# Stores in 8 KB rows, a written order for every engine, and 29 gate products on GpSimd in a scan and mixture-of-adapters kernel

## The chip, the core and the metric

The kernel runs on one core of a Trainium2 chip. The core has TensorE (PE, matrix products; PEld is its loading of weights), VectorE (DVE), ScalarE (ACT), GpSimd (POOL), SyncE (SP, which here only issues DMAs) and 16 DMA engines. The metric is the device time of one execution in microseconds (us), the median of several runs. A profile is one execution; its span goes from the first to the last instruction.

## The reference

Eight sequences of 6400 rows of 128 numbers go through a linear recurrence. The resulting 51200 rows go through a mixture of eight rank-16 adapters, of which the two with the largest gate logits are used.

```python
for t in range(S):                       # a, b: [8, 6400, 128]
    h = a[:, t] * h + b[:, t]
    out[:, t] = h
...
x = out.reshape(51200, 128)
logits = x @ w_gate                      # [51200, 8]
topk = np.argpartition(-logits, K, axis=1)[:, :K]      # K = 2
w = softmax of the two selected logits
...
delta[mask] += w[mask, k, None] * (x[mask] @ A[e]) @ B[e]
...
return x + delta
```

Everything is float32 outside; 26.2 MB each of a, b and output.

## The kernel before

The 51200 rows are cut into 100 units of 512 rows. Each unit goes through these steps; the letters are the names of the operations in the code.

- **ld** (SyncE): a and b come in by DMAs of two units each, 128 partitions by 4 KB, into rings `a_in` and `b_in` of eight slots. A slot is loaded again when the transposes of its units are done.
- **AB** (TensorE, function `transposes`): eight float32 transposes each of a and b on half the partitions, into `pA` and `pB`, so that time runs along the free dimension.
- **aev** (ScalarE, L491): `pA` is copied to `a_st`. Then **scan** (VectorE, L510): one scan instruction makes x for 512 steps, in float16, into the ring `xT`, and starts from the last column of the unit before.
- **L** (TensorE): gate logits, four matmuls of 8 columns into a part of the bank `pTL`. For a group of up to four units **lev** (ScalarE) copies them out, VectorE reduces (L618, L646: the two largest), GpSimd does the elementwise steps (L625 to L674), and **sig** (ScalarE) makes the gate weights `g`.
- **Z** (TensorE): x times all A, into `pZ`. **mul** (L729): Z times the gate, on VectorE from `pZ`, or, for the units that `POOL_MULS` names, on GpSimd from `z_sb`, to which ScalarE has copied Z first (**zev**, L715). Result `zw`, float16.
- **T** (TensorE): transposes `zw` into the other part of `pTL`. **tev** (ScalarE, L786) copies it to `zwT`.
- **R** and **D** (TensorE, function `delta`): into `pO`, x itself (as weights against an identity) and then `zwT` times B.
- **oev** (ScalarE, some of the last ones VectorE, L821): `pO` goes to one of the `NOUT` = 24 slots of `outt`.
- **st** (SyncE): two units' slots go out in one DMA of 128 rows of 4 KB; units 0, 1 and 96 to 99 one at a time, in rows of 2 KB. So that a row of the output holds eight consecutive input rows, R reads every eighth column of x over two units (`x_rows`) and tev rearranges its columns to match (`evacuated`). A store also waits for the scan 22 units later (`HOLD`), so that loads go first.

The tiles that limit how far the steps can run ahead: `xT` holds 16 units, `zwT` two tiles of two units, `pB`, `pZ` and `pO` two each, `pA` one.

The order of instructions on each engine is made by `_Plan.schedule` at build time: a list scheduler with an estimated cost of each operation, offsets for its kind (`KEY`) and a tolerance (`SLACK`). It also picks the engine where there is a choice. Each engine runs its list strictly in order, and `run` (L188) puts semaphore waits ahead of an operation where another engine's work is needed. All DMAs but those of the constants are in SyncE's list. In the steady part the planner comes to T, L, D, Z, R, AB on TensorE for every unit.

Of the kernel before, what the change touches and what calls it, by code (L numbers as in the profile page):

```python
# [5 lines left out]
ALU = mybir.AluOpType  # L6
ACTF = mybir.ActivationFunctionType
F32 = mybir.dt.float32
# [4 lines left out]
KEY = {  # L13
    "AB": -228.9, "aev": 79.1, "scan": 140.1, "L": -12.2, "lev": -63.6, "gate": 83.5, "sig": 69.7, "Z": 27.8,
    "mul": -75.3, "zev": 6.2, "T": -117.7, "tev": 38.1, "R": 189.8, "D": 29.2, "oev": 168.4,
}
SLACK = {"pe": 20.0, "dve": 20.0, "act": 0.0, "pool": 60.0, "sp": 120.0}
# [3 lines left out]
POOL_MULS = (2, 10, 4, 2)  # L21
# [3 lines left out]
WIDE = 100  # L25
SOLO = (2, 4)
FUSE = (100, 100)
WIDE8 = 460.0
RING = 8
XR = 16  # L30
NOUT = 24
TAIL = 10
FILLS = 1


class _Op:


    def __init__(self, name, engs, kind, unit, cost, emit, deps, dma, bank, mode):
        self.name = name  # L40
        self.engs = engs
        self.eng = engs[0]
        self.kind = kind
        self.unit = unit
        self.cost = cost
        self.emit = emit
        self.deps = deps
        self.dma = dma
        self.bank = bank
        self.mode = mode  # L50
        self.signal = False
        self.done = None
# [7 lines left out]


# [30 lines left out]
class _Plan:  # L92


    def __init__(self, sems, offset, slack):
        self.sems = sems
        self.offset = offset
        self.slack = slack
        self.ops = {}
        self.order = {e: [] for e in sems}  # L100

    def add(self, name, eng, kind, unit, cost, emit, deps=(), dma=None, bank=None, mode=None):

        engs = (eng,) if isinstance(eng, str) else eng
        cost = cost if isinstance(cost, dict) else {e: cost for e in engs}
        self.ops[name] = _Op(name, engs, kind, unit, cost, emit, list(deps), dma, bank, mode)

    def schedule(self, first, link, landing, switch):
        ops = self.ops
        users = {n: [] for n in ops}  # L110
        left = {}
        for op in ops.values():
            op.deps = [ops[d] for d in dict.fromkeys(op.deps) if d in ops]
            left[op.name] = len(op.deps)
            op.key = op.unit + self.offset.get(op.kind, 0.0)
            op.quick = min(c[0] for c in op.cost.values())
        for op in ops.values():
            for d in op.deps:
                users[d.name].append(op)
        begin, end = {}, {}  # L120
        cand = {e: [] for e in self.sems}
        free = {e: first for e in self.sems}
        bank = {}
        mode = None
        for op in ops.values():
            if not left[op.name]:
                for e in op.engs:
                    cand[e].append((0.0, op))
        todo = len(ops)
        while todo:  # L130
            found, soonest = [], {}
            for e, c in cand.items():
                for x in c:
                    op = x[1]
                    t = max(free[e], x[0])
                    if op.bank:
                        for o in bank.get(op.bank, {}).values():
                            if o.eng != e:
                                t = max(t, end[o.name])
                    if op.mode and mode and op.mode != mode:  # L140
                        t = max(t, free[e] + switch)
                    t += op.cost[e][0] - op.quick
                    found.append((t, op, e, x))
                    if t < soonest.get(e, 1e18):
                        soonest[e] = t
            e0 = min(soonest, key=soonest.get)
            limit = soonest[e0] + self.slack.get(e0, 0.0)
            t, op, e, pick = min((f for f in found if f[2] == e0 and f[0] <= limit), key=lambda f: (f[1].key, f[0]))
            t -= op.cost[e][0] - op.quick
            for x in op.engs:  # L150
                cand[x].remove(pick)
            op.eng = e
            mode = op.mode or mode
            if op.bank:
                held = bank.setdefault(op.bank, {})
                op.deps += [o for o in held.values() if o.eng != e]
                held[e] = op
            self.order[e].append(op)
            begin[op.name] = t
            free[e] = t + op.cost[e][0]  # L160
            if op.dma:
                ready = free[e] + 1000.0
                wait = max(0.0, link - ready)
                link = max(link, ready) + op.dma[2]
                end[op.name] = link + 300.0 + min(wait, landing(link))
            else:
                end[op.name] = t + op.cost[e][1]
            todo -= 1
            for u in users[op.name]:
                left[u.name] -= 1  # L170
                if not left[u.name]:
                    for x in u.engs:
                        cand[x].append((max(end[d.name] for d in u.deps), u))
        self.begin, self.end = begin, end
        self.span = max(end.values())
        for op in ops.values():
            for d in op.deps:
                d.signal = True
        for e, seq in self.order.items():
            n = 0  # L180
            for op in seq:
                if op.dma:
                    op.done = op.dma[:2]
                else:
                    n += op.signal
                    op.done = (self.sems[e], n)
# [18 lines left out]
def bass_associative_scan_2x2__then__mixture_of_adapters_kernel(  # L205
# [20 lines left out]
    lo, hi, every, at = POOL_MULS  # L226
    ON_POOL = lambda v: lo < v < NU - hi and v % every == at
# [22 lines left out]
    with ExitStack() as stack:  # L250
# [15 lines left out]
        A_e = sb(nc.sbuf_tensor("A_e", [E, D * R], F32))  # L266
# [29 lines left out]
        s_cst = sb(nc.semaphore("s_cst"))  # L296
        dma_sem = {}

        plan = _Plan(sems, KEY, SLACK)
        add = plan.add  # L300

        def add_dma(name, eng, unit, starts, slot, time, deps=()):
# [11 lines left out]
            add(name, eng, "dma", unit, (450.0 * len(starts), 0.0), emit, deps, (sem, value, time))  # L314


        add("id0", "pool", "fix", -109, (200.0, 450.0), lambda h: h.memset(ident_f[:, :], 0.0))
# [3 lines left out]
            "fix",  # L321
            -109,
            (300.0, 400.0),
# [9 lines left out]
            ["id0"],  # L333
        )

        def cst_load(name, dst, src, after):

            sem = sb(nc.semaphore(f"s_{name}"))
            add(
                name,  # L340
                "act",
                "fix",
                -109,
                (450.0, 0.0),
                lambda h: h.dma_start(dst, src).then_inc(sem, 16),
                after,
                (sem, 16, 100.0),
            )
# [9 lines left out]
        add("w0", "dve", "fix", -109, (60.0, 200.0), lambda h: h.memset(warm[:, :], 0.0))  # L358
        add("table", "act", "fix", -108, (1500.0, 1600.0), lambda h: h.activation(warm[:, :], warm[:, :], ACTF.Sigmoid), ["w0"])
        add("wt", "dve", "fix", -109, (270.0, 400.0), lambda h: h.memset(warm_t[:, :], 0.0))  # L360
# [6 lines left out]
        add("heat", "pe", "fix", -109, (372.0 * HEATS, 372.0 * HEATS), heat, ["wt"], mode="half")  # L367

        def fill(w):


            def emit(h):
                for _ in range(3):
                    last = h.matmul(pO[1][:, :], warm_t[:, 0:128], warm_t[:, :])
                return last

            add(f"fill{w}", "pe", "fix", 1000.0, (600.0, 800.0), emit, [f"AB{w}"])

        for w in range(FILLS):
            fill(w)  # L380
        add("idh", "dve", "fix", -108, (150.0, 330.0), lambda h: h.tensor_copy(ident_h[:, :], ident_f[:, :]), ["id"])
        add("cstg", "pool", "fix", -108, (190.0, 290.0), lambda h: h.tensor_copy(wg_h, cst_f[:, 0:E]), ["ld_g"])
        add(
            "cstA",
            "pool",
            "fix",
            -107,
            (290.0, 390.0),
            lambda h: h.tensor_copy(Acat_h, cst_f[:, E : E + 128]),
            ["ld_A"],  # L390
        )
        add(
            "cstB",
            "pool",
            "fix",
            -106,
            (290.0, 390.0),
            lambda h: h.tensor_copy(Bcat_h, cst_f[:, E + 128 : E + 256]),
            ["ld_B"],
        )  # L400

# [525 lines left out]
```

## Time and profile before

| | before |
|---|---|
| median of 3 runs | 204.45 us (204.28 to 204.6) |
| profiled execution, device time | 204.28 us |
| its span | 202.5 us |
| TensorE busy | 191.0 us (94%) |
| VectorE busy | 184.7 us (91%) |
| ScalarE busy | 174.0 us (86%) |
| GpSimd busy | 115.7 us (57%) |
| moved by DMA | 79.35 MB, 392 GB/s on average |

In the rows of the profile a group of instructions has its line, engine and operation, the tile it writes and those it reads, partitions by elements, "x" with its count, then busy us and mean ns of one, then the idle time of the engine before them with what ended most of it. In the 40 slices each digit is the busy share in tenths. A row of the DMA queues has packets, megabytes, and packet time as a share of the 16 engines' span. Matmuls overlap in the pipeline, so that a single one lasts longer than it holds the engine; VectorE's and ScalarE's instructions overlap a little as well, and start to start is what one holds.

### The profile page before, as it was taken

Reading aid. Unit: us, or ns where it says so; the run is one execution under the profiler, and the core shown is the slowest. Engines: PE = TensorE matmul, PEld = TensorE weight load, DVE = VectorE, ACT = ScalarE, POOL = GpSimd, SP = SyncE. Lnnn points to the kernel's source line nnn. Section 1 sums busy time; section 2 is a strip of 40 time slices with the busy share of each in tenths; the row PEclk is TensorE's granted clock in tenths of the full one; section 3 lists DMA queues with packets and bytes.
Section 4 is the critical chain, followed back from the end, with each engine's and each line's share of the span. In section 5 each row is a group of like instructions: output and inputs, shape, how many; then the busy total and the mean of one; then the engine's idle time right before and its main releaser. Section 6 shows DMA issues by size and latency. Waiting matters only on the chain.

```text
span 202.5 us, 8763 instructions
## 1 busy us (share of the span) xinstructions
PE 191.0 (94%) x3594; PEld 171.4 (85%) x3594; DVE 184.7 (91%) x268; ACT 174.0 (86%) x383; POOL 115.7 (57%) x244
## 2 busy tenths in 40 slices
PE   7888988899999999999999999999999999999982
PEld 3666777789899999999999999999999999998981
DVE  1699989999999999999999999999999999988970
ACT  2366775969999999999999999999999999999882
POOL 1325337668467565656746656565674687865620
PEclk9999999999999999999999999999999999999999
DMA  7999999999999999999999999999999999988866
GB/s 185 401 408 409 406 408 406 403 406 411 403 413 414 410 419 409 409 411 414 412 416 409 414 413 411 411 415 415 409 412 414 413 414 410 385 350 350 324 271 263
DMA packets 23687, 79.35 MB, mean 392 GB/s; under 512 B 3680, under 2 KB 3808, under 8 KB 23648
## 3 DMA queue, kind: packets, MB, share of 16 engines
q1 hardware_dynamic: 22320, 78.65, 97.3%
q8 instruction: 29, 0.48, 1.0%
q10 hardware_dynamic: 1328, 0.14, 0.5%
q14 instruction: 10, 0.08, 0.1%
HBM read 52.56 MB, written 26.21 MB: 389 GB/s over the span
## 4 chain that ended last, share of the span: by engine, by line
PE 84%; ACT 6%; DVE 5%; issue 2%; POOL 1%; DVEq 0%
PE pA L86 27%; PE pO L82 23%; PE pTL L86 14%; PE pZ L82 10%; PE pTL L82 5%; DVE xT L510 4%; PE pB L86 4%; ACT a_st L491 2%; ACT outt L821 2%; PE pB L82 2%; ACT zwT L786 1%; DVE mx L589 1%; ACT Lg L583 0%; ACT z_sb L715 0%; POOL pn L632 0%
## 5 line engine op out<-in xcount | busy, mean ns | idle before, releaser
L510 DVE TENSOR_TENSOR_SCAN xT<-a_st,xT,pB 128x512 f16<-128x512 f32 x96 | 120.1, 1251 | 3.2 <-ACT zwT L786 0.5
L491 ACT COPY a_st<-pA 128x512 f32<-128x512 f32 x100 | 60.6, 606 | 19.2 <-PE pB L86 14.6
L86 PE MATMUL pA<-ident_f,a_in 64*128 64x64 f32 (+1 forms) x792 | 71.8, 230 | 2.5 <-ACT a_st L491 0.7
L86 PE MATMUL pB<-ident_f,b_in 64*128 64x64 f32 (+1 forms) x792 | 71.9, 230 | 0.3 <-issue 0.2
L86 PEld LDWEIGHTS pA<-ident_f,a_in 64*128 64x128 f32 (+1 forms) x792 | 57.9, 139 | 10.9 <-ACT a_st L491 1.9
L821 ACT COPY outt<-pO 128x512 f32<-128x512 f32 x96 | 59.5, 626 | 1.9 <-PE pO L82 1.7
L786 ACT COPY zwT<-pTL 128x512 f16<-128x512 f16 x95 | 58.4, 615 | 1.0 <-PE pTL L86 1.0
L86 PEld LDWEIGHTS pB<-ident_f,b_in 64*128 64x128 f32 (+1 forms) x792 | 57.5, 138 | 1.0 <-issue 0.7
L729 DVE TENSOR_TENSOR zw<-pZ,g 128x512 f16<-128x512 f32 x79 | 53.2, 679 | 2.4 <-PE pTL L86 1.4
L82 PE MATMUL pO<-ident_h,xT 128*128 128x128 f16 x400 | 40.8, 227 | 0.9 <-ACT outt L821 0.9
L86 PE MATMUL pTL<-ident_h,zw 128*128 128x128 f16 x380 | 37.8, 221 | 0.5 <-ACT zwT L786 0.4
L82 PE MATMUL pZ<-cst_h,xT 128*128 128x128 f16 x400 | 38.1, 219 | 0.0
L82 PE MATMUL pO<-cst_h,zwT 128*128 128x128 f16 x400 | 36.8, 218 | 0.5 <-ACT zwT L786 0.4
L82 PEld LDWEIGHTS pO<-ident_h,xT 128*128 128x128 f16 x400 | 32.5, 147 | 1.5 <-ACT outt L821 1.2
L729 POOL TENSOR_TENSOR zw<-z_sb,g 128x512 f16<-128x512 f32 x21 | 22.3, 1060 | 17.8 <-PE pTL L82 17.3
L82 PE MATMUL pTL<-cst_h,xT 128*128 128x8 f16 x400 | 27.5, 174 | 1.4 <-DVE xT L510 1.3
L82 PEld LDWEIGHTS pZ<-cst_h,xT 128*128 128x128 f16 x400 | 27.8, 114 | 0.1
L86 PEld LDWEIGHTS pTL<-ident_h,zw 128*128 128x128 f16 x380 | 21.8, 98 | 6.7 <-ACT zwT L786 0.5
L625 POOL TENSOR_TENSOR d<-Lg,m 128x128 f32<-128x128 f32 (+3 forms) x29 | 10.7, 369 | 26.6 <-DVE m L618 26.5
L82 PEld LDWEIGHTS pTL<-cst_h,xT 128*128 128x128 f16 x400 | 23.5, 117 | 2.6 <-DVE xT L510 2.0
L82 PEld LDWEIGHTS pO<-cst_h,zwT 128*128 128x128 f16 x400 | 23.8, 98 | 1.0 <-PE pO L82 0.9
L660 POOL TENSOR_SCALAR pn<-d 128x128 f32<-128x128 f32 (+3 forms) x31 | 17.3, 557 | 2.7
(38 smaller groups left out, 138.3 us busy)
## 6 DMA issues: line engine op xcount, KB each, us to landing
a_in<-in_a_dram SPq DMA_DIRECT2D x49, 512.0 KB, 14.4
b_in<-in_b_dram SPq DMA_DIRECT2D x49, 512.0 KB, 14.2
out_dram<-outt SPq DMA_DIRECT2D x47, 512.0 KB, 13.9
out_dram<-outt SPq DMA_DIRECT2D x6, 256.0 KB, 3.0
a_in<-in_a_dram SPq DMA_DIRECT2D x2, 256.0 KB, 9.1
b_in<-in_b_dram SPq DMA_DIRECT2D x2, 256.0 KB, 4.1
cst_f<-in_moe_A_dram ACTq DMA_DIRECT2D x1, 64.0 KB, 4.2
cst_f<-in_moe_B_dram ACTq DMA_DIRECT2D x1, 64.0 KB, 4.9
```

What stands on the lines that cost most here:

```text
L82: return self.h.matmul(*args, **kw)
L86: return self.h.transpose(*args)
L491: lambda h: h.copy(a_st[w % 2][:, :], pA[0][:, :]),
L510: last = h.tensor_tensor_scan(out=x_at(lo, hi), data0=a_st[w % 2][:, lo:hi], data1=pB[w % 2][:, lo:hi], initial=init, op0=ALU.mult, op1=AL ...
L589: last = h.max(mx[s][:, j, :], Lg[s][:, j, :])
L625: lambda h: h.tensor_tensor(out=v(d1[s]), in0=v(Lg[s]), in1=bc(m1[s]), op=ALU.subtract),
L660: lambda h: h.tensor_scalar(v(pn[s]), v(d2[s]), 0.0, -1.0e30, ALU.is_lt, ALU.mult),
L729: lambda h: h.tensor_tensor(out=oview, in0=zview, in1=gview, op=ALU.mult),
L786: lambda h: h.copy(*evacuated(v)),
L821: return copy(outt[:, v % NOUT, :], pO[v % NO][:, :])
```

## The change

Four things change together.

- Units 8 to 87 form groups of four: one store of 128 rows of 8 KB for each. Output rows then hold sixteen consecutive rows, so R reads every sixteenth column of x over four units, tev rearranges over four, and `zwT` has four units to a tile. R and D of a unit need the scans of its whole group, and D the tevs.
- The planner goes. `ORDERS` gives the order of each engine, one letter for an operation; the n-th occurrence of a letter is the n-th operation of its kind. `BANKS` gives the order of use of the shared banks, and `ELSE` the operations that take the other engine.
- `POOL_MULS` names 29 units, every third from 4 to 88, in place of 21 (every fourth from 6 to 86).
- `outt` has 36 slots instead of 24, `xT` 20 instead of 16. The three filler matmuls after the first unit and an unused tile go.

What each instruction computes is the same, as are the loads, the hold of 22 scans, and the gate's steps. Letters: a AB, A the a part of a unit that is loaded alone, c aev, s scan, L, l lev, Z, z zev, u mul, T, t tev, R, D, o oev, m and n the two reductions, x the sort of the first groups, g sig, i and j loads, w a store.

```diff
+ORDERS = {
+    "pe": """
+        hAaALaaZLaZRaLRLaZTLaDLaTZaDaTLZLLaZaTZRaTLLDaRDLLaTZaRRDaTDZRaLTLLLaZZDaLTRaRTDZaLTZLLaZRTaZTDDaLLT
+        RaDZZRaLDTLRaRZLTaZLTDaLTDRZaLZTRDaLTDZRaTDZRaLZDTLLRaRTDZaTDRZaLZLDTaRTLDLaZRTZRaZDDLTaRZLTDaZTLRLa
+        ZRDTaDRZTaDZRLTaDZTRLLLaRDZTaDZTRaDRZTLDaRLTLDRLaDZZTRaDTZRaLDTZRaDZLTLLaZRTRDaDLTZRaDTRZaDTZLLLRaDT
+        ZRaTRZDaLTLZDaRTZDaTLRLZaRDTLZDaRTLDZaZTLRLaRDZDTaRZTDaRZLTLDaRTLZLDaRTZDZRaTDRZaLLTDRaDZLTLaRZRTaZD
+        DTLaRZTDZRaLTLDRaZLTDRaDTZRaZTLDRaZDTRLaDZLLTaZRTRaZDDTLaRZLTaZDLTLRaRLDTZDaTZRZRDLDLTaRZTDaRZTLDRaL
+        TDZaZRLTaDRLTZaZDRTaDRZLTLaZDRTaZRLTDaDTLLRLZDRZDTARRDDaTLRRDZDZLTRTZDRZTDTRZDRDZTRTDZRTDRZDZTRDRTDT
+        RDRD
+    """,
+    "dve": """
+        qvysxssxu4s7sxsmusnmsususnmssnsusmsusnsusmsusnsususmsusnsusmsusnususmsusnsumsusnsususmsusnusmsusunss
+        musussnusmussusunssmususnusmsusnsususmsususnsumsusnumsussnsusumsusnsususmsusnsusumssunsusmusmnusnsum
+        susnmsusunsmsumsusnnsumusnuuumouunuououuo
+    """,
...
+    "sp": """
+        ijijjjijijjijjiiijijjijijiiijiijjjiiiiwjjwijjjjijwwjijjiiiijjiiwwijiwjiwjiiiiwjjjiiiwjjjwijwijijwwii
+        jjjjiiiiwijjwjjwjwiiwwwwwwwwwwwwwwwe
+    """,
...
-POOL_MULS = (2, 10, 4, 2)
+POOL_MULS = (4, 7, 10, 13, 16, 19, 22, 25, 28, 31, 34, 37, 40, 43, 46, 49, 52, 55, 58, 61, 64, 67, 70, 73, 76, 79, 82, 85, 88)
...
-SOLO = (2, 4)
-FUSE = (100, 100)
-WIDE8 = 460.0
+FILL = ()
+PAIRS = (2, 96)
+QUADS = (8, 88)
+SINGLE = 100
 RING = 8
-XR = 16
-NOUT = 24
+XR = 20
+NOUT = 36
 TAIL = 10
-FILLS = 1
...
+    def arrange(self):
+        ops = list(self.ops.values())
+        for op in ops:
+            op.deps = [self.ops[d] for d in dict.fromkeys(op.deps) if d in self.ops]
+        self.order = {e: self.pick(ORDERS[e], [op for op in ops if op.eng == e]) for e in self.sems}
...
-        zwT = [sb(nc.sbuf_tensor(f"zwT{i}", [128, 2 * UT], F16)) for i in range(2)]
+        zwT = [sb(nc.sbuf_tensor(f"zwT{i}", [128, 4 * UT], F16)) for i in range(2)]
...
-        solo = set(range(SOLO[0])) | set(range(NU - SOLO[1], NU))
+        def length(v):
+            return 4 if QUADS[0] <= v < QUADS[1] else 2 if PAIRS[0] <= v < PAIRS[1] else 1
...
         def mates(v):
-            return [v] if v in solo else [v // 2 * 2, v // 2 * 2 + 1]
+            n = length(v)
+            return list(range(v // n * n, v // n * n + n))
...
-            dst = zw_tile(v)[:, :].rearrange("c (h q u m) -> c u h q m", h=2, q=Q, u=2)[:, v % 2]
-            return dst, t_dst(v).rearrange("c (q m h) -> c h q m", q=Q, h=2)
...
+            dst = zw_tile(v).rearrange("c (h q u m) -> c u h q m", h=n, q=Q, u=n)[:, v % n]
+            return dst, t_dst(v).rearrange("c (q m h) -> c h q m", q=Q, h=n)
...
-            x0 = v % XR // 2 * 2 * UT
-            return xT[:, x0 : x0 + 2 * UT].rearrange("d (m i) -> d i m", i=QI)[:, v % 2 * Q + q, :]
+            n = length(v)
+            x0 = (v // n * n) % XR * UT
+            return xT[:, x0 : x0 + n * UT].rearrange("d (m i) -> d i m", i=n * Q)[:, v % n * Q + q, :]
...
-                [f"T{v}"] + [f"D{w}" for w in mates(v - 4)],
+                [f"T{v}"] + [f"D{w}" for m in mates(v) for w in mates(m - 8)],
...
-            stores.append((u, len(mates(u))))
-            u += stores[-1][1]
+            n = max(length(u), 2 if u < NU - SINGLE else 1)
+            stores.append((u, n))
+            u += n
...
-            rows = out[u0 * UT : (u0 + n) * UT, :].rearrange("(p i) d -> p (i d)", p=128)
+            rows = out[u0 * UT : (u0 + n) * UT, :]
+            dst, src = rows.rearrange("(n p i) d -> p n (i d)", p=128, i=Q), outt[:, s0 : s0 + n, :]
+            if length(u0) == n > 1:
+                dst, src = rows.rearrange("(p i) d -> p (i d)", p=128), src.rearrange("p n c -> p (n c)")
...
-        plan.schedule(700.0, 3000.0, lambda t: 400.0, 94.0)
+        plan.arrange()
```

More of the change, by code (lines that the diff above doesn't have):

```diff
@@ L92, with __init__ @@
 class _Plan:
-    def __init__(self, sems, offset, slack):
+    def __init__(self, sems):
         self.sems = sems
-        self.offset = offset
-        self.slack = slack
         self.ops = {}
[L100 to L176, printed above, removed]
@@ L312, in emit @@
                 return last
[L314 to L317 removed]
+            add(name, eng, emit, deps, (sem, value))
+        add("idz", "pool", lambda h: h.memset(ident_f[:, :], 0.0))
         add(
@@ L569, in bc, with step @@
                 return t[:, 0:c].to_broadcast([128, c, E])
-            def step(name, eng, time, emit, deps):
-                if isinstance(time, str):
-                    time = cost(time)
-                    time = {e: time[e] for e in ((ge,) if isinstance(ge, str) else ge)}
-                add(f"{name}_{k}", eng, "gate", u, time, emit, deps)
+            def step(name, eng, emit, deps):
+                add(f"{name}_{k}", eng, emit, deps)
             add(
```

268 lines of the change are left out of this document (97 added, 171 removed).

## The prediction

> **What bounds the kernel now.** I read the page's totals and its 40 slices first, then the busy time by stretches, the chain of waits inside one steady unit, VectorE's order of instructions, and the stores.
>
> ```profile
> span 202.5 us, 8763 instructions
> PE 191.0 (94%) x3594; PEld 171.4 (85%) x3594; DVE 184.7 (91%) x268; ACT 174.0 (86%) x383; POOL 115.7 (57%) x244
> ...
> DMA  7999999999999999999999999999999999988866
> ...
> q1 hardware_dynamic: 22320, 78.65, 97.3%
> q8 instruction: 29, 0.48, 1.0%
> q10 hardware_dynamic: 1328, 0.14, 0.5%
> ```
>
> No engine has slack worth naming except GpSimd, and the DMA row is full for 35 of its 40 slices. By stretches (the columns are us from the start, then busy us of each engine, clock, DMA share, GB/s):
>
> ```profile
> core 0: us, PE busy (x) PEld busy (x) DVE busy (x) ACT busy (x) POOL busy (x), PEclk, DMA share, GB/s
> 5.00:175.00 170.00, 164.57 (x3206) 148.89 (x3205) 164.05 (x233) 150.81 (x334) 102.50 (x206) 1.00 1.03 410
> 175.00:190.00 15.00, 14.73 (x261) 13.53 (x259) 13.67 (x22) 14.10 (x34) 10.04 (x26) 1.00 0.90 358
> 190.00:197.00 7.00, 6.54 (x112) 6.34 (x110) 5.78 (x11) 5.64 (x12) 2.30 (x7) 1.00 0.66 257
> 197.00:201.00 4.00, 1.39 (x18) 0.88 (x15) 0.61 (x1) 1.92 (x4) 0.00 (x0) 1.00 1.00 378
> ...
> 57.60:175.00 117.40, 117.31 (x2339) 108.42 (x2338) 115.12 (x154) 112.50 (x249) 75.04 (x142) 1.00 1.03 412
> ```
>
> So two things run side by side. The DMA engines are full (share 1.03, neighbouring packets overlap a little) from 5 to 175 us, when the last loads are in. From 175 to 197 they idle for part of the time, 0.10 x 15 + 0.34 x 7 = 3.9 us, because the outputs they wait for are not made yet; from 197 to 201 they are full again. And TensorE is busy for 117.31 of 117.40 us from 57.6 us on. One unit of it, from the chain:
>
> ```profile
> 99.91 0.33 PE pTL L86 x4
> 100.24 0.11 PE pTL L82 x4
> 100.34 0.24 PE pO L82 x4
> 100.59 0.22 PE pZ L82 x4
> 100.81 0.26 PE pO L82 x4
> 101.07 0.20 PE pA L86
> ...
> 101.72 0.33 PE pTL L86 x4
> ```
>
> In order T, L, D, Z, R and the 16 input transposes AB: 1.81 us from one T to the next (101.72 - 99.91). VectorE's own cycle is as long, which is why neither shows a long wait:
>
> ```profile
> 100.88 1.27 DVE L510 TENSOR_TENSOR_SCAN xT<-a_st,xT,pB 128x512 f16<-128x512 f32 x1
> 102.08 0.69 DVE L729 TENSOR_TENSOR zw<-pZ,g 128x512 f16<-128x512 f32 x1
> 102.69 0.28 DVE L618 TENSOR_REDUCE m<-Lg 128x16 f32<-128x128 f32 x1
> 102.88 1.27 DVE L510 TENSOR_TENSOR_SCAN xT<-a_st,xT,pB 128x512 f16<-128x512 f32 x1
> ```
>
> From start to start a scan holds VectorE 1.20 us, a gate product 0.61, a reduction 0.19. The end is the last eviction and its store:
>
> ```profile
> 198.57 0.58 ACT L821 COPY outt<-pO 128x512 f32<-128x512 f32 x1 [0.16 <-PE pO L82]
> ...
> DMA to landing us min/median/max: 2.4/3.1/5.2
> ```
>
> The second row is for the eight stores issued from 189.8 us on. The last one takes 2.4 us, so 199.2 + 2.4 = 201.6 us. The earlier ones still take up to 5.2 us while the mean DMA share is 0.66, which says that some of the 16 engines still have a backlog while others have none. **DMA and computation end together**: a gain needs both, and the smaller of the two gains is what the clock shows.
>
> **The DMA part.** Stores of units 8 to 87 go from 40 DMAs of 128 rows of 4 KB to 20 of 128 rows of 8 KB. The bytes stay. Gone are 40 x 128 - 20 x 128 = 2560 rows and 20 x 16 = 320 completion packets, 2880 of q1's 22320. What one packet costs beside its bytes is not shown by itself. From above: q10's packets, 0.5% x 202.5 x 16 / 1328 = 12.2 ns each for 105 bytes; q1 moves 78.65 MB in 97.3% x 202.5 x 16 = 3152 us, 25 bytes per ns, so 105 bytes are 4 ns and 8 ns are left. 2880 x 8 / 16 engines = **1.4 us**. With all 12.2 ns it is 2.2 us. From below: q8's packets are the only longer ones (16.5 KB), and at 1.0% x 202.5 x 16 / 29 = 1.1 us they go at no better rate per byte, so a longer packet may save nothing: 0. A loss I leave to the slower cases: q8 moves instructions, one packet at a time, and no row shows data in rows over 4 KB. I take 1.4, by the many small packets of the data's own kind. The Trainium skill ("DMA: Bandwidth & Descriptors", section "Why small descriptors are slow (HBM only)") gives about 3 cycles of overhead per packet; at the 850 MHz of that page this is 3.5 ns, and 2880 of them over 16 engines would be an estimate of 0.6 us instead.
>
> The rest of this part is free. A store of four units waits for the slowest of four evictions, but stores were held back for 22 scans anyway (HOLD stays), and 36 slots instead of 24 cover the longer wait; if they did not, ScalarE's eviction would wait for a store, which the waits of before never show. SyncE issues 33 stores instead of 53, at its written places among the loads; a load behind a late store would wait, with over ten us of queued transfers as cover.
>
> **The compute part.** Eight gate products move from VectorE to GpSimd (21 to 29):
>
> ```profile
> L729 POOL TENSOR_TENSOR zw<-z_sb,g 128x512 f16<-128x512 f32 x21 | 22.3, 1060 | 17.8 <-PE pTL L82 17.3
> ...
> L715 ACT COPY z_sb<-pZ 128x512 f32<-128x512 f32 x21 | 13.3, 632 | 0.0
> ```
>
> GpSimd gains 8 x 1.06 = 8.5 us on 115.7, in a span of 202: off the path. ScalarE gains 8 evictions of at most 0.63 us = 5.1 on 174.0: no longer free (a rival below). VectorE loses 8 x 0.61 = 4.9 us. Not all of that is gain, since TensorE is full from 57.6 us on. What counts is how early TensorE can become full, and what is left to do then. The 57.6 us are the start of unit 30's input transposes. VectorE had done by the scan of unit 30 (59.5 us):
>
> ```profile
> L729 DVE TENSOR_TENSOR zw<-pZ,g 128x512 f16<-128x512 f32 x17 | 11.3, 672 | 0.2 <-PE pTL L86 0.2
> ...
> L618 DVE TENSOR_REDUCE m<-Lg 128x16 f32<-128x128 f32 (+2 forms) x8 | 2.0, 244 | 0.0
> L646 DVE TENSOR_REDUCE m<-L 128x16 f32<-128x128 f32 (+2 forms) x7 | 1.6, 235 | 0.0
> ```
>
> 17 products and 15 reductions. The written order of VectorE has 15 and 14 ahead of that scan, and two small gate steps of about 0.1 us fewer: 2 x 0.61 + 0.19 + 0.2 = **1.6 us earlier**. TensorE had done by 57.6 us, in matmuls (four to a unit):
>
> ```profile
> L82 PE MATMUL pZ<-cst_h,xT 128*128 128x128 f16 x84 | 7.7, 220 | 0.0
> ...
> L82 PE MATMUL pO<-ident_h,xT 128*128 128x128 f16 x68 | 6.7, 228 | 0.3 <-ACT outt L821 0.3
> L82 PE MATMUL pO<-cst_h,zwT 128*128 128x128 f16 x64 | 5.2, 218 | 0.4 <-ACT zwT L786 0.4
> ```
>
> 21 Z, 17 R, 16 D. The written order of TensorE has 20, 15 and 14 ahead of AB of unit 30 (L and T are equal): 0.22 + 2 x 0.26 + 2 x 0.24 = **1.2 us owed** later. From there the pieces of the cycle add up to 0.33 + 0.11 + 0.24 + 0.22 + 0.26 + 0.20 + 7 x 0.06 = 1.78 of 1.81 us. Over the 65 units up to 175 us the other 0.03 come to 2.0 us of small waits on a VectorE just as long. With VectorE at 71 products instead of 79 I take half of it back: **1.0 us**; bounds 0 and 2.0. The tail I leave as it is. Sum: 1.6 - 1.2 + 1.0 = 1.4 us (0.4 to 2.4).
>
> Three edits at nothing: the three filler matmuls go (they ran while TensorE waited for the second unit); xT has 20 slots, so a scan that waits for a group of four is still covered (15 R are done by AB of unit 30, and its scan needs 12); the eviction of zw reads PSUM at twice the stride, off the path, at most some ns on 0.6 us.
>
> R reads xT with a stride of 32 bytes in place of 16, as weights:
>
> ```profile
> L82 PEld LDWEIGHTS pZ<-cst_h,xT x400: 111/113/133, 7.9 to 194.3; 128*128 128x128 f16 x134
> L82 PEld LDWEIGHTS pO<-ident_h,xT x400: 111/148/175, 8.2 to 197.8; 128*128 128x128 f16 x134
> L82 PEld LDWEIGHTS pO<-cst_h,zwT x400: 95/96/107, 14.2 to 198.3; 128*128 128x128 f16 x134
> ```
>
> These are strides of 8, 16 and 2 bytes: 113, 148 and 96 ns. Bounds for 32 bytes: 148 again (the price is per element that sits alone in what is fetched, and at 16 that is already so), or 148 + 16 x 35 / 8 = 218. I take 148 as the likelier; 218 is a rival. The Trainium skill ("SBUF — State Buffer", section "Door 1") says SBUF is read in lines of 16 bytes and each new line is paid for. By that rule, every element is a new line at 16 and at 32 bytes alike, and R costs nothing more. The trace agrees as far as it goes: 8 bytes, two to a line, are cheap.
>
> **The sum.** Both sides give 1.4 us. The profiled execution took 204.28 us with a span of 202.5; 204.28 - 1.4 = **202.9 us**. The three runs have their median at 204.45, so this is 0.8% below.
>
> **The rivals.**
>
> R's weights (slower). The place is TensorE's steady cycle. From 113 to 148 ns, four loads cost 0.14 us more, and R takes 0.04 more than Z (0.26, 0.22), so 0.04 of 0.14 came through. From 148 to 218 the same share is 4 x 70 x 0.04 / 0.14 = 0.08 us, in 80 units 6.4 us; all of it would be 22. Time: 202.9 + 6.4 = 209.3. It decides from 1.4 / 80 = 18 ns per R on. For it: the rise over three strides. Against it: the 16-byte step already separates all elements.
>
> ScalarE becomes the bound (slower). In the middle it is busy for 112.50 of 117.40 us. About 65% of the eight new evictions fall there: 5 x 0.63 = 3.3 us, which leaves 1.6. If an order written for it waits anywhere by more, the 1.6 us are not won while the 1.2 are owed, and the tail is longer by what the written order has behind the last AB:
>
> ```profile
> 187.20:202.50 15.30, 10.57 (x168) 9.72 (x168) 8.98 (x16) 10.08 (x22) 4.40 (x11) 1.00 0.74 286
> ```
>
> 42 groups of four after unit 99's scan begins, against 48 there: about 6 x 0.24 = 1.4 us. Time: 204.28 + 1.4 = 205.7. Against it: its busy time counts overlap.
>
> The rows save nothing (no change). If the lagging DMA engines set the end and an 8 KB row costs two of 4 KB, only 320 completion packets go, 0.2 us: 204.1. For it: q8; against it: q10.
>
> The tail closes (faster). The 3.9 us of idle DMA from 175 to 197 are there because the outputs come late. If the written tail brings them earlier by half, 1.9 us come on top: 201.0. Against it: TensorE is busy for 14.73 of 15 and 6.54 of 7 us there.
>
> **How the numbers follow.** The likeliest case 0.54, its own range 201.9 to 203.9; R's weights 0.07; ScalarE 0.12; no saving 0.13; the tail 0.14. From 201.0 to 205.2 leaves out R's weights, part of ScalarE and half of the faster case. A difference under 0.2% (0.4 us) cannot be told from none. Faster 0.71 (0.54 + 0.14 + some of no saving), same 0.10, slower 0.19.
>
> **What would show it.** Right: q1 at about 22320 - 2880 = 19440 packets with a share times span shorter by 1.4 us; unit 30's scan at about 58 us; TensorE still full behind it; R's weight load at about 148 ns; GpSimd's product x29. Wrong: R's weight load at 170 ns or more; waits of TensorE on a_st or zwT evictions in the middle; waits of ScalarE on a store; q1's packet time unchanged; the last eviction after 199 us.

## The result and the profile after

The changed kernel takes 206.72 us (median of four runs, 206.53 to 206.92) against 204.52 for the kernel before: ratio 1.011, 95% interval 1.009 to 1.013. The forecast was 202.9 us with a range up to 205.2; it was wrong in sign. The profiled run took 206.71 us. From its page (totals, slices, queues, groups; PEclk is the clock that TensorE was granted, in tenths of full speed):

```profile
span 204.9 us, 8755 instructions
PE 193.9 (95%) x3591; PEld 173.4 (85%) x3591; DVE 179.3 (88%) x258; ACT 180.9 (88%) x392; POOL 124.7 (61%) x254
...
PEclk9759999999999999999999999999999999999997
DMA  6999999999999999999999999999999999977985
GB/s 170 402 410 406 407 408 404 403 405 409 414 406 408 352 309 398 408 413 417 408 409 409 393 402 409 410 427 405 407 412 411 421 422 412 418 309 298 405 354 202
...
q1 hardware_dynamic: 19440, 78.65, 96.1%
...
L614 POOL TENSOR_TENSOR zw<-z_sb,g 128x512 f16<-128x512 f32 x29 | 30.8, 1063 | 26.6 <-ACT z_sb L608 18.0
...
L115 PEld LDWEIGHTS pO<-ident_h,xT 128*128 128x128 f16 x400 | 33.1, 149 | 1.5
```

VectorE is 5.4 us less busy, ScalarE 6.9 more and GpSimd 9.0 more; R's weights cost 149 ns at a stride of 32 bytes, as at 16. The packets went as counted, to 19440. Two things are new. The clock row has a stretch at half speed (0.50 from about 8 to 14 us), where the kernel before has none; more on that below. And the GB/s row has two slices of 352 and 309 at 66 to 77 us, where the kernel before has over 400. In a table by stretches (us from the start, busy us of PE, PEld, DVE, ACT, POOL, then clock, DMA share, GB/s), first before, then after:

```profile
66.00:72.00 6.00, 6.00 (x122) 5.60 (x118) 5.88 (x10) 5.95 (x14) 3.67 (x7) 1.00 1.03 413
72.00:78.00 6.00, 6.00 (x127) 5.53 (x125) 5.89 (x10) 5.76 (x14) 3.45 (x7) 1.00 1.03 413
180.00:185.00 5.00, 4.89 (x92) 4.51 (x91) 4.50 (x8) 4.62 (x11) 2.12 (x6) 1.00 0.91 366
```

```profile
66.00:72.00 6.00, 6.00 (x119) 5.43 (x118) 5.79 (x9) 5.82 (x12) 3.92 (x7) 1.00 0.92 356
72.00:78.00 6.00, 6.00 (x123) 5.51 (x122) 5.76 (x9) 5.97 (x15) 3.22 (x6) 1.00 0.93 324
180.00:185.00 5.00, 4.92 (x98) 4.40 (x96) 4.76 (x8) 5.00 (x12) 3.87 (x10) 1.00 0.65 265
```

So the DMA engines lose 0.11 x 6 + 0.10 x 6 = 1.3 us in the middle, although loads and stores were free to go there, as the next lines show. SyncE's timeline of the kernel after shows what was issued when (start, duration, transfer, how many in a row):

```profile
58.88 0.85 SPq L287 DMA_DIRECT2D out_dram<-outt  x2
62.17 0.34 SPq L287 DMA_DIRECT2D b_in<-in_b_dram  x1
62.56 0.45 SPq L287 DMA_DIRECT2D a_in<-in_a_dram  x1
65.99 3.87 SPq L287 DMA_DIRECT2D b_in<-in_b_dram  x2
69.89 2.03 SPq L287 DMA_DIRECT2D a_in<-in_a_dram  x4
73.21 3.96 SPq L287 DMA_DIRECT2D b_in<-in_b_dram  x2
77.21 0.93 SPq L287 DMA_DIRECT2D a_in<-in_a_dram  x2
78.24 0.87 SPq L287 DMA_DIRECT2D out_dram<-outt  x2
```

No store is issued for 19 us (59.35 to 78.24), and four a loads come at once at 69.89. The written order has `iiiijjiiwwiji...` there. SyncE takes its order one by one: the first of those a loads was free to go at 56.6 us (its ring slot had been read), but stood behind a b load whose slot came free only at 69.5. The store of units 8 to 11 was free to go at 59.2 us, when the scan it is held for ended:

```profile
57.94 1.27 DVE L433 TENSOR_TENSOR_SCAN xT<-a_st,xT,pB 128x512 f16<-128x512 f32 x1
```

It went 19 us later, as the second of the two stores at 78.24. Later in the run stores are up to 24 us late (units 24 to 27: free at 88.6, behind a load that was free at 112.4).

The end is again the last eviction and its store. In the kernel after the evictions of units 98 and 99 (ScalarE's timeline), and the stores issued from 190 us on:

```profile
199.52 1.28 ACT L692 COPY outt<-pO 128x512 f32<-128x512 f32 x2
...
DMA to landing us min/median/max: 3.5/4.4/6.5
```

The last eviction ends at 200.8 instead of 199.2, and the store behind it lands after 3.5 us instead of 2.4. Both are later by more than a us.

### The profile page after: what moved, and what is told of

It reads as the page before. It is cut to its first block, busy times and chain, and to the rows that moved or that the text cites. A ratio compares the mean times of both kernels' runs of the same rounds, so it can differ in the third digit from the quotient of the medians.

```text
span 204.9 us, 8755 instructions
## 1 busy us (share of the span) xinstructions
PE 193.9 (95%) x3591; PEld 173.4 (85%) x3591; DVE 179.3 (88%) x258; ACT 180.9 (88%) x392; POOL 124.7 (61%) x254
## 3 DMA queue, kind: packets, MB, share of 16 engines
q1 hardware_dynamic: 19440, 78.65, 96.1%
## 4 chain that ended last, share of the span: by engine, by line
PE 87%; DVE 3%; DMA 3%; issue 2%; ACT 2%; SPq 1%; ACTq 0%
PE pA L119 27%; PE pO L115 26%; PE pZ L115 12%; PE pTL L119 11%; PE pTL L115 6%; PE pB L119 4%; DVE xT L433 3%; DMA b_in<-in_b_dram 3%; SPq L287 1%; ACT a_st L414 1%; ACT outt L692 1%; ACT zwT L663 0%; ACT Lg L488 0%; DVE zw L614 0%; DVE m L545 0%
## 5 line engine op out<-in xcount | busy, mean ns | idle before, releaser
L119 PE MATMUL pA<-ident_f,a_in 64*128 64x64 f32 (+1 forms) x792 | 73.3, 232 | 3.2 <-DMA a_in<-in_a_dram 1.0
L119 PE MATMUL pB<-ident_f,b_in 64*128 64x64 f32 (+1 forms) x792 | 74.0, 233 | 0.3 <-issue 0.2
L119 PEld LDWEIGHTS pB<-ident_f,b_in 64*128 64x128 f32 (+1 forms) x792 | 58.9, 141 | 1.2 <-issue 0.5
L663 ACT COPY zwT<-pTL 128x512 f16<-128x512 f16 x95 | 57.4, 605 | 1.6 <-PE pTL L119 0.8
L614 DVE TENSOR_TENSOR zw<-pZ,g 128x512 f16<-128x512 f32 x71 | 47.6, 674 | 3.9 <-PE pZ L115 1.5
L614 POOL TENSOR_TENSOR zw<-z_sb,g 128x512 f16<-128x512 f32 x29 | 30.8, 1063 | 26.6 <-ACT z_sb L608 18.0
L115 PE MATMUL pO<-ident_h,xT 128*128 128x128 f16 x400 | 43.0, 232 | 0.0
L115 PE MATMUL pZ<-cst_h,xT 128*128 128x128 f16 x400 | 39.3, 222 | 0.0
L115 PE MATMUL pO<-cst_h,zwT 128*128 128x128 f16 x400 | 38.2, 220 | 0.7 <-POOL d L504 0.2
L115 PEld LDWEIGHTS pO<-ident_h,xT 128*128 128x128 f16 x400 | 33.1, 149 | 1.5
L115 PEld LDWEIGHTS pZ<-cst_h,xT 128*128 128x128 f16 x400 | 27.6, 115 | 1.8
L115 PEld LDWEIGHTS pO<-cst_h,zwT 128*128 128x128 f16 x400 | 24.7, 98 | 3.1 <-PE pO L115 1.1
L115 PE MATMUL pTL<-cst_h,xT 128*128 128x8 f16 x400 | 25.7, 175 | 0.6 <-issue 0.3
L119 PEld LDWEIGHTS pTL<-ident_h,zw 128*128 128x128 f16 x380 | 23.9, 98 | 1.6 <-issue 0.6
L115 PEld LDWEIGHTS pTL<-cst_h,xT 128*128 128x128 f16 x400 | 21.9, 117 | 2.4 <-DVE xT L433 0.6
```

The source lines that it names most:

```text
L115: return self.h.matmul(*args, **kw)
L119: return self.h.transpose(*args)
L614: add(f"mul{v}", eng, lambda h: h.tensor_tensor(out=oview, in0=zview, in1=gview, op=ALU.mult), deps)
L663: lambda h: h.copy(*evacuated(v)),
```

## The experiments

Each is the kernel before or after with one thing done or undone; ratios are to the kernel before, with their 95% interval.

**One part of the change alone, under the kernel before's planner.**

```diff
 e1_planner_rest: before.py, planner kept
+POOL_MULS = (...)      29 units
+QUADS = (8, 88)        rows of 8 KB, with length(), mates(), zw_tile(), x_rows() as in the change
+XR = 20, NOUT = 36
 e2_rows_alone: rows of 8 KB and XR = 20 only
 e3_29_alone:
-POOL_MULS = (2, 10, 4, 2)
+POOL_MULS = (3, 10, 3, 1)
```

> All of the change but the written order: rows of 8 KB, 29 products on GpSimd, 36 and 20 slots, and the list scheduler of before makes the order. If the written order is the loss (TensorE has weights with a stride behind AB and some waits, SyncE leaves the DMA engines short at 66 to 80 us), this is back at 203.5 to 204.8 us, a unit lasts 1.80 to 1.82 us from unit 30 to 95, and the DMA share is 1.0 until the last load. If the rows or the 29 products are the loss, it stays at 206 us or more.

> The kernel before with the rows of 8 KB over four units alone (xT and zwT as large as they need), planner, 21 products, 24 slots. If a row of 8 KB costs the DMA engines as much as two of 4 KB, and grouping costs nothing: 204.0 to 204.8 us. If groups of four make the outputs late: over 205.5 us. My prediction's price of a row would give 203.1 us.

> The kernel before with the 29 products on GpSimd alone. If VectorE limits the first 57 us, unit 30's scan starts 1 to 1.5 us earlier than 59.5 and the time is 203.0 to 204.2 us; the DMA engines, full until the last load, leave at most that. If ScalarE becomes the bound through eight more evictions: 205 us or more.

Measured: e1 216.57 us, 1.060 (1.057 to 1.063); e2 221.81, 1.085 (1.083 to 1.088); e3 211.90, 1.037 (1.034 to 1.040). None says what the part is worth: with the offsets left as they were, the planner lost the round T L D Z R AB that it has found for the set of before. In e1 TensorE's order became, with `a` for AB, `LDaTZZRRDTLZaTLRZaTDD`. Offsets fitted to one set of operations don't carry to another, so a written order and the operations that it orders can't be judged apart in this way.

**One part undone in the written order.**

```diff
 e4_pairs_written: after.py
-QUADS = (8, 88)
+QUADS = (100, 100)
 and each store of four in SyncE's order becomes two of two at the same place (w -> ww)
 f4_21_written: after.py, the products of units 7, 19, 28, 40, 49, 61, 70, 82 back on VectorE behind their Z
```

> The changed kernel with its written order, but rows of 4 KB over two units again (two stores stand where one of four units stood). If the rows are not the loss: 206.2 to 207.2 us, as with 8 KB. If the groups of four are: 204.5 us or less.

> The changed kernel with 21 products on GpSimd: 8 of the 29 go back to VectorE behind their Z, and their evictions leave ScalarE; all other orders stay. If the 8 evictions make ScalarE late: 205.8 us or less. If VectorE's relief is what lets the scans run: 207.5 us or more, and a unit lasts longer than 1.86 us.

Measured: e4 206.92 us, 1.013 (1.011 to 1.016): the rows are not what made the kernel slow. Its profile (206.29 us) parts the two ways of being late. No stop of TensorE that is put down to "issue" (the engine waits for nothing that the profile shows) is over 0.2 us in it between 20 and 190 us, and the last eviction ends where that of the kernel before does, at 198.59 + 0.59 = 199.18 us, but the last store takes 4.6 us to land, not 2.4. The stores from 188 us on:

```profile
DMA to landing us min/median/max: 4.6/5.4/7.6
```

With SyncE's written order the transfers end late even when the computation doesn't. f4: 210.04 us (208.32 to 211.37), 1.024 (1.020 to 1.027): the written order is made for its 29 products; its profile also has stops of TensorE of 0.9 and 2.8 us that are put down to "issue", so its size isn't read further.

**SyncE's order, TensorE's order, both.** In f1 the entries of SyncE from the 27th on are sorted by when each was free to go in the trace of after; nothing else changes. In f2 in 33 places a T or D that was ready is put first behind AB, as in the kernel before. f3 has both.

```diff
 f1_sync_order: after.py, "sp"
-...iijjjiiiiwjjwijjjjijwwjijjiiiijjiiwwijiwjiwjiiiiwjjj...
+...iijijijijijijijiwwjwijwijwijwijijwijijwijijwijijwij...
```

> The changed kernel, SyncE's order alone changed: from its 27th entry on, loads and stores stand in the order in which the trace of after has them ready (a slot of the ring is free; the outputs are made and the scan of 22 units later is done), where the written order issues loads up to 13 us and stores up to 24 us late. If the DMA engines that lag set the end (the last store takes 3.5 us instead of 2.4): 205.4 to 206.0 us, and the DMA share is 1.0 in 60 to 80 us where it is 0.97. If TensorE's order sets the end: 206.5 us or more.

> The changed kernel, TensorE's order alone changed: in 33 places a D or T that is ready comes first behind AB, in place of R, Z or L, whose weights are read with a stride. From the trace of after a group behind AB lasts 240 ns for R, 195 for Z, 123 for L against 190, 168 and 97 elsewhere, while D and T lose 10: about 0.9 us less on TensorE. If TensorE sets the end: 205.6 to 206.0 us. If the DMA engines do: 206.4 to 206.8 us.

> Both of these orders together. If the two limits stand side by side, as I think: 204.6 to 205.4 us, lower than either alone. If one of them alone sets the end, this equals the better of the two.

Measured: f1 204.38 us, 1.000 (0.998 to 1.001); f2 206.99, 1.013 (1.010 to 1.017); f3 205.49, 1.005 (1.003 to 1.006). SyncE's order is worth the 2.3 us by itself, more than I had expected. TensorE's is worth nothing as I changed it, and with SyncE's order mended it costs 1.1 us (f3 against f1), where I had expected f3 to be the fastest. In f1's trace, the span and q1 from the page, and the two stretches, are

```profile
span 202.3 us, 8755 instructions
...
q1 hardware_dynamic: 19440, 78.65, 96.7%
...
66.00:72.00 6.00, 6.00 (x122) 5.59 (x119) 5.79 (x9) 5.82 (x12) 3.53 (x7) 1.00 1.03 420
72.00:78.00 6.00, 6.00 (x127) 5.51 (x125) 5.76 (x8) 5.97 (x15) 3.59 (x6) 1.00 1.02 410
```

and the end is that of the kernel before: units 98 and 99 evicted by 199.18 us, the last store landed 2.6 us after its issue.

```profile
197.89 1.29 ACT L692 COPY outt<-pO 128x512 f32<-128x512 f32 x2
...
DMA to landing us min/median/max: 2.6/3.2/5.1
```

**Which of SyncE's entries.** g1 keeps the loads in their written order and moves only the stores to when they are free; g2 sorts the loads and leaves each store behind as many loads as it was.

> The changed kernel with the loads in the written order and each store moved to where its outputs are ready. If the stores that stand up to 24 us late are the loss (the DMA engines have nothing to do at 66 to 80 us): 204.3 to 205.0 us. If it is the loads: 206.2 us or more.

> The changed kernel with the loads in the order in which their slots come free, and the stores behind as many loads as written. If a load that waits for its slot and holds back others that could go is the loss: 204.3 to 205.0 us. If it is the late stores: 206.2 us or more. If both halves are needed, both this and the run before it lie between 205 and 206.2.

Measured: g1 204.41 us, 1.000 (0.998 to 1.001); g2 204.48, 1.001 (0.998 to 1.003); both have a DMA share of 1.02 or 1.03 at 60 to 80 us. Either set mended is enough: in these kernels the DMA engines run dry at that place only when a late load and a late store come together.

**Slots and rows with SyncE's order mended.**

```diff
 g3_24_slots: f1 with
-NOUT = 36
+NOUT = 24
 g4_pairs_ready: f1 with
-QUADS = (8, 88)
+QUADS = (100, 100)
```

> The order of SyncE that gave 204.38 us, with 24 output slots instead of 36. If the 36 slots do nothing once the stores go when they are ready: 204.1 to 204.8 us, and no eviction waits for a store. If groups of four need them: 205 us or more, with ScalarE's evictions waiting.

> The order of SyncE that gave 204.38 us, with rows of 4 KB over two units instead of 8 KB over four. If a row costs by its bytes alone (q1 takes 3150 us of engine time after, 3152 before): 204.1 to 204.8 us. If 8 KB rows save what I predicted (1.4 us): 205.2 us or more. If the groups of four delay the outputs: under 204.0 us.

Measured: g3 204.51 us, 1.000 (0.999 to 1.002): twelve more slots do nothing. g4 205.04, 1.004 (1.001 to 1.007), 0.66 us above f1, with intervals that touch. Part of the 0.66 may be TensorE's clock: its mean over the execution was under 0.99 in ten of g4's twelve executions and in five of f1's, and the medians of the others (two and seven) are 0.25 us apart. The time that q1's packets take is read more sharply from the pages, as share times span. Rows of 4 KB (g4):

```profile
span 203.3 us, 8803 instructions
...
q1 hardware_dynamic: 22320, 78.65, 96.9%
```

That is 0.969 x 203.3 = 197.0 us for each engine, and 0.973 x 202.5 = 197.0 in the kernel before; f1, with rows of 8 KB, has 0.967 x 202.3 = 195.6, and the other kernels with its rows and a mended SyncE (f3, g1, g2, g3) have 195.4 to 196.0. The rows save 1.0 to 1.6 us of every DMA engine's time. The written order takes about as much away: the kernel after has 0.961 x 204.9 = 196.9. Against e4, which has the same order and rows of 4 KB (0.970 x 204.5 = 198.4), its rows save 1.5. The count of packets doesn't settle this time alone: e2, f4 and h3, with rows of 8 KB in kernels that are slower for other reasons, have 197.8, 198.7 and 201.8. So the saving is read best from pairs that differ in the rows and little else (f1 and g4, after and e4).

**The kernel before's own round, written down.** These put the operations of before in its own order of every engine (TensorE's round T L D Z R AB kept), and then the products, or the rows, into it. All of them, i1 and i3 too, have the three filler matmuls of before again.

```diff
 h2_21_cycle: after.py with QUADS = (100, 100), ORDERS and BANKS as the planner of before made them
 h1_29_cycle: the same, 29 products, each in GpSimd's order by the time at which VectorE had begun it
 h3_29_cycle_rows: h1 with
+QUADS = (8, 88)
 and the orders of TensorE, ScalarE and SyncE arranged for groups of four
```

> The same with the kernel before's 21 products: nothing of the change but 36 output slots, 20 slots of x and the order put down in writing. Both theories: the time of before, 204.3 to 204.8 us, and unit 30's scan at 59.5 us. If this is faster or slower by over 0.3 us, then slots or the writing down count for themselves and h1_29_cycle is read against this run.

> The kernel before's own order of every engine, written out (TensorE keeps the fixed round T L D Z R and the two inputs' transposes in the steady part), with the 29 gate products of the kernel after on GpSimd (each with its copy on ScalarE), 36 slots, 20 slots of x and rows of 4 KB. Theory (VectorE's relief is real, and the irregular order of TensorE in the kernel after gives it back): unit 30's scan near 57.6 us as in f1_sync_order, and then the pitch of before, 1.815 us a unit, not 1.837: 65 x 0.022 = 1.4 us less than f1_sync_order, so 202.7 to 203.2 us. Rival (the relief is given back by the products themselves: GpSimd's 1063 ns and the copy are late for the transpose behind them, whatever the order): a pitch of 1.837 or more and 204.4 us or above.

> h1_29_cycle with rows of 8 KB over four units, where the result's second half waits for four units' copies, so that TensorE's round is broken in about half of the units (T L D Z R, then T L Z R, then T L Z D D R). Theory: an irregular round costs, 0.2 to 1.4 us more than h1_29_cycle (203 to 204.4 us). Rival (irregularity costs nothing, rows of 8 KB save up to 0.6 us): 0 to 0.6 us less than h1_29_cycle.

Measured: h2, the control, 207.67 us, 1.016 (1.014 to 1.018); h1 210.08, 1.029 (1.027 to 1.031); h3 242.95, 1.189 (1.187 to 1.191). h3 shows that the rows need another round: R and D of four units wait for one another's copies, which its waits name ("PE pO L115 <- ACT zwT L663: 14.9, 21, 1.7": us, times, longest). The control was to be as fast as before and is 3.3 us slower, with its last eviction under 0.5 us later. The place is at 180 to 190 us:

```profile
180.00:185.00 5.00, 4.96 (x95) 4.49 (x94) 4.58 (x7) 4.64 (x11) 2.59 (x8) 1.00 0.44 170
185.00:190.00 5.00, 4.84 (x75) 4.47 (x73) 4.96 (x8) 4.72 (x12) 3.51 (x7) 1.00 0.48 189
```

A letter stands for the next operation of its kind, so the stores of h2 go by unit. Those of units 72 to 77 are held for the scans of units 94, 96 and 98. The planner had let the stores of units 78 to 83, which are held for nothing, past some of them; in h2 they stand behind. The last three kernels release units 72 and on from the hold.

```diff
 i1_21_cycle_free: h2 with      i2_sync_order_free: f1 with
-FREE = 100
+FREE = 94
 i3_27_cycle_free: i1 with 27 products: every third unit from 4 to 76, then 82 and 86
```

> h2_21_cycle with one number changed: stores of units 72 to 77 no longer wait for the scan 22 units on (FREE 94 in place of 100). In h2_21_cycle the stores stand in SyncE's order by unit, those of units 72 to 77 wait for the scans of units 94, 96 and 98, and the stores of units 78 to 87, which wait for nothing, stand behind them; the kernel before has them ahead. Theory (a store that waits at the head of SyncE's order is what cost h2_21_cycle its 3.3 us: 0.44 and 0.48 of the DMA engines' time at 180 to 190 us, and the backlog then outlasts the last eviction): the DMA share there back to 0.85 or more, and the time of before, 204.0 to 204.8 us. Rival (slots, or the writing down): 207 us or more.

> f1_sync_order with the same number changed: the stores of units 72 to 79 don't wait for scans 94 and 98. In f1_sync_order the DMA engines had 0.40 of their time at 180 to 185 us, yet the backlog was all but gone by the last eviction (199.18 us, landing 2.6 us after its issue). Theory: only the landing of the last store can gain, 2.6 to 2.0 us: 203.7 to 204.4 us. Rival (the loads' end and the units behind it gain too): 203 us or less.

> i1_21_cycle_free with 27 products on GpSimd: every third unit up to 76, then 82 and 86 as before, since in h1_29_cycle the products of units 79, 85 and 88 held GpSimd's gate steps, and through them VectorE's, in the last rounds. Theory (TensorE sets the pitch in its fixed round, and VectorE's relief is worth nothing there: from the first scan to unit 30's it was 53.41 us in h1_29_cycle and 53.37 in h2_21_cycle; the 2.0 us at unit 30 of f1_sync_order are copies and result products that TensorE puts off, 1.4 us of them by its own group times): within 0.5 us of i1_21_cycle_free. Rival (VectorE's relief is real and h1_29_cycle lost it in its last rounds alone): 1.5 us or more below i1_21_cycle_free.

Measured: i1 204.54 us, 1.001 (1.000 to 1.001), with its DMA engines at work again in the first of the two stretches:

```profile
180.00:185.00 5.00, 4.97 (x95) 4.50 (x93) 4.58 (x7) 4.64 (x12) 2.35 (x7) 1.00 0.97 389
185.00:190.00 5.00, 4.83 (x75) 4.46 (x73) 4.96 (x9) 4.71 (x12) 3.50 (x7) 1.00 0.72 288
```

One number, and 3.1 us are back: a store that waits at the head of SyncE's order is enough to set the end of a kernel whose computation ends in time. i2: 204.35, 0.999 (0.998 to 1.001); f1's backlog was small enough to be caught up, and the gap moves: the DMA share at 180 to 185 us rises from 0.40 to 0.70, that at 185 to 190 falls from 1.01 to 0.56. i3: 205.31, 1.004 (1.003 to 1.006), 0.8 us above i1, further off than I had expected, and to the slow side: six products fewer on VectorE win nothing in this order, where TensorE keeps its round. No kernel here is faster than the one before.

## Why the prediction was wrong, point by point

**The step that failed** is the sentence "SyncE issues 33 stores instead of 53, at its written places among the loads; a load behind a late store would wait, with over ten us of queued transfers as cover", under "The rest of this part is free". I looked at one load behind one store and not at the string as it stands: its runs of `iiii` and `jjjj` make loads wait for loads, and stores behind them by up to 24 us. Cover of ten us is used up by lateness of 13 and 19. It cost 206.72 - 204.38 = 2.3 us, which f1, g1 and g2 each give back. No load came late to TensorE for it: by the trace of after each load from unit 20 on has landed 3.4 us or more before its unit's transposes begin. The loss is DMA time. The transfers end later, as e4 shows with its computation in time, and the end is theirs. In the profile of after the last eviction is 1.6 us late as well; 0.8 us of that are two stops of TensorE (0.46 us at 78.4, 0.35 at 116.2) that the profile puts down to "issue", and 0.4 was there at unit 30, behind the stretch with TensorE's clock at 0.50. The trace has one thing at the stops: the packets of q8, the queue of instructions, start 5.7 to 6.6 us apart between 44 and 169 us but for two, at 76.3 and 113.8, which come 7.2 us behind the one before, and each stop ends 1.6 us after such a packet is through. So instructions that came late behind SyncE's bursts are the likeliest cause, but no run tests it; e4, with the same bursts, has neither the late packets nor the stops.

**DMA, 1.4 us.** The size was right: 22320 packets became 19440, and 197.0 us of each engine became 195.4 to 196.0 where SyncE's order is mended. (The DMA row of before is full in 34 of its 40 slices, not in 35; nothing hangs on that.) That is (1.0 to 1.6) x 16 / 2880 = 6 to 9 ns a packet, about the 8 ns taken from q10. The rule of the Trainium skill ("DMA: Bandwidth & Descriptors", section "Why small descriptors are slow (HBM only)"), which made it 0.6 us by my estimate, falls short of these runs. But DMA and computation end together, as the prediction said, and only the smaller gain shows.

**Computation, 1.6 - 1.2 + 1.0.** VectorE's 1.6 came: unit 30's scan begins at 57.55 us in f1 (57.94 in after) and at 59.54 before, 2.0 us ahead in f1 and 1.6 in after. So did the 1.2 that TensorE owes. By the groups from the start to that scan, before and then f1 (matmuls, four to a unit):

```profile
L82 PE MATMUL pZ<-cst_h,xT 128*128 128x128 f16 x88 | 8.1, 220 | 0.0
L82 PE MATMUL pO<-ident_h,xT 128*128 128x128 f16 x72 | 7.1, 228 | 0.3 <-ACT outt L821 0.3
L82 PE MATMUL pO<-cst_h,zwT 128*128 128x128 f16 x68 | 5.6, 218 | 0.4 <-ACT zwT L786 0.4
```

```profile
L115 PE MATMUL pZ<-cst_h,xT 128*128 128x128 f16 x84 | 8.0, 222 | 0.0
L115 PE MATMUL pO<-ident_h,xT 128*128 128x128 f16 x64 | 6.7, 229 | 0.0
L115 PE MATMUL pO<-cst_h,zwT 128*128 128x128 f16 x60 | 5.7, 219 | 0.3 <-POOL d L504 0.2
```

One Z, two R and two D are left for later: 0.22 + 2 x 0.26 + 2 x 0.24 = 1.2 us. What failed is the third term. I took half of the 0.03 us a unit of small waits as won, 1.0 us; instead the units from 30 to 95 take 119.4 us in f1 (57.55 to 176.98) against 118.0 before (59.54 to 177.52), 1.4 us more. Of that only the Z, 0.2 us, is work put off: by unit 95's scan f1 has 348 matmuls of Z, 324 of R and 320 of D behind it, before has 348, 332 and 328. The last evictions end together, at 199.18 and 199.16, so the gain of this part is 0.0, not 1.4: in the prediction's terms 2.0 - 1.2 - 0.8, with -0.8 us in the place of the third term's 1.0. TensorE's irregular order may be what takes it: 1.837 us a unit against 1.815, with R in f1 lasting 304 ns from its start to the next group's right behind AB and 256 elsewhere (at 60 to 165 us, where AB doesn't follow), while before has T behind AB in every round, which in f1 takes 234 there and 223 elsewhere. f2 and f3, which move T and D there in 33 places, did not win it back, so this reading isn't shown, and the cause of this part stays open. i3 against i1 has no gain from VectorE's relief under the fixed round either.

**The sum** by the prediction's own rule is then a gain of the smaller of 1.4 and 0.0, so the time of before, which is what f1 has (204.38); what SyncE's order costs, 2.3 us, comes on top.

**The edits at nothing and the rivals.** The 36 slots are indeed worth nothing (g3), and no wait of ScalarE on a store shows. R's weights: refuted, 149 ns. ScalarE as the bound, 205.7: its row is the nearest in time but not in cause; TensorE's waits in after show no ScalarE row above 0.8 us. The rows save nothing: their DMA time is saved, what they save of the whole is at most 0.66 us (g4 against f1). The tail closes: it opened, to 0.65 of the DMA engines' time at 180 to 185 us against 0.91 before. There the stores of units 72 to 79 are held for scans 94 and 98 with all others behind them, but i2, without that hold, gains nothing. No rival named SyncE's order, and the range ended 1.5 us below the result.

The three filler matmuls may not be at nothing. In all nine profiles of kernels that have them (before, e1 to e3, h1 to h3, i1, i3) TensorE's clock is 1.00 over the first 16 us. In seven of the eleven without (after, e4, f3, f4, g1, g4, i2) it is 0.50 for 3.4 to 10.2 us from about 8 to 10 us on. In the profiles of g1 and i2, which have f1's order of TensorE, unit 30's scan then begins at 58.77 and 58.80 us against 57.55 in f1, and the last eviction ends at 200.43 and 200.48 against 199.18. Over all executions of the five kernels with that order and a mended SyncE (f1, g1 to g3, i2) it is less: a median of 204.5 us where the mean clock was under 0.99, 204.3 elsewhere. It doesn't explain the 2.3 us: the kernel after took 206.72 and 206.71 at a mean clock of 0.976 and 0.977, 206.92 and 206.53 at 0.992 and 0.995. No run adds the fillers alone.

## What to carry to other kernels

A DMA queue fed by one engine in a written order is a chain of waits of its own: for each entry set the time at which it is free to go beside the time at which those ahead of it are, and see whether loads and stores are late together; the cover in transfers under way has to outlast the longest such wait. Where transfers and computation end together, price both and take the smaller gain, and count work that is only put off (a scan 2 us earlier with 1.2 us of products still owed) as a loan. An order fitted to one set of operations is part of that set: parts put under the old order came out slower in every try here (e1, e2, e3, h1, h3, i3), and so did the 29 products taken back to 21 in the new one (f4), while the rows and the slots came out of it with little change (e4, g3, g4).

## What the hardware showed that was not expected

A packet of q1 costs 6 to 9 ns beside its bytes even between rows of 4 and 8 KB, in pairs of kernels that differ in little else, small as that is against some 160 ns for the 4 KB. TensorE's weights cost the same at strides of 16 and 32 bytes (147 and 149 ns), and less at 8 and 2 (115 and 98): the Trainium skill ("SBUF — State Buffer", section "Door 1") has a price for each new line of 16 bytes, and these rows agree in that 16 and 32 bytes cost the same and the most; but the Trainium skill has full bandwidth there from two accesses to a line on, and here 8 bytes, two to a line, still cost 17 ns more than 2. TensorE can stop for 0.35 to 2.8 us in the middle of a group with nothing that releases it in the profile (after and f4). Three of these four stops end 1.6 us after a late packet of the queue of instructions (7.2 us behind the one before in after, 8.5 in f4), the one of 2.8 us doesn't; no run here tested what they wait for.
